# Expert weights in a routed two-layer network: one read and one kept copy of the last 64 rows of w1

## The chip, the core and the metric

The kernel runs on one core of a Trainium2 chip. The metric is device time in microseconds (us), the median over runs. The engines in the text are TensorE (PE, with its weight loads as PEld), VectorE (DVE), ScalarE (ACT), GpSimd (POOL) and SyncE (SP, which only issues transfers here). "DMA" is the core's 16 transfer engines together.

## The reference, cut to what matters

```
out  = causal 7-tap convolution of x per head (weights: softmax of `weight`)     # 28672 tokens x 192
logits = out @ w_gate                                                            # 8 experts
every token goes to one expert, greedily by logit, at most 3584 tokens an expert
for e in range(8):
    h = max(out[of e] @ w1[e], 0)        # w1[e]: 192 x 1024
    y[of e] = h @ w2[e]                  # w2[e]: 1024 x 192
```

All of it is float32. The kernel keeps float32 accuracy by splitting each operand in a high part (what TensorE's float32r format holds) and a low part (the rest), and by adding up several products of the parts.

## The kernel before

The program has two stages that overlap in time. First the convolution runs over 16 half batches (`conv`, tiles `X`, `cv`, `a`), its result is stored in DRAM (`attn`), and the gate's logits are formed (`aT`, `pl` or `bg`, `L`, `LT`). Then the two-layer network runs over 56 tiles of 512 tokens (`FFN.run`), while the routing of later tiles (thresholds, sorting, lists) goes on in the background, placed between the matmuls by a planner (`Pace`, `Steps.hook`), which counts a rough cost for each instruction that is written, and writes background steps where VectorE and ScalarE seem free.

A tile needs its expert's weights. `plan` writes the order of the pieces. The first eight tiles are one for each expert, and there each expert's weights are read from the inputs in eight pieces: `a` (rows 0 to 127 of w1, 512 columns at a time, two pieces), `d` (rows 128 to 191, two pieces), `w` (w2, four pieces). `wload` issues the read of one piece into one of four `raw` buffers. `wsplit` takes one piece: ScalarE writes the high part, VectorE (GpSimd for the four pieces that are split during the convolution) subtracts to get the low part, SP issues stores of both parts into DRAM (`kept1`, `keptd`, `kept2`; `kw`, `kd`, `kv` in the profile), and the read of the next piece is issued. So four pieces are under way at any time. Later tiles of the same expert do not split again: `W1` and `W2` read the kept parts back (16 times each), into the weight tiles `w1` and `dl` and into `w2` (the profile calls both weight tiles `w`).

The 64 last rows of w1 are held twice. TensorE's fourth matmul of a group has the high part of these rows in partitions 0 to 63 and again in 64 to 127 (`W[:, 2]`), because the moving operand `xd` has the tokens' high part in the lower half and their low part in the upper half. The fifth uses `dl`, the low part, whose upper half is zero. Before the change the doubling is done by reading the rows twice, into both halves of the `raw` buffer.

All transfers of weights are issued by SP, in the order in which they are written, each after what it waits for. The stores of `attn` are issued by ScalarE, gathers of tokens (`xg`) and scatters of results by GpSimd.

In a tile, step f does one group of five matmuls of layer one (`l1`, into one of three `ph` banks), ScalarE's `hh` and VectorE's `hl` empty the bank, then half a block of layer two of the tile before (`l2`), then one piece of `wsplit`.

Of the kernel before, what the change touches and what calls it, by code (L numbers as in the profile page):

```python
# [6 lines left out]
F32 = mybir.dt.float32  # L7
# [3 lines left out]
AF = mybir.ActivationFunctionType  # L11
# [4 lines left out]
NE, D, NTOK, F, CAP = 8, 192, 28672, 1024, 3584  # L16
W, HW_, NHB = 112, 16, 16
# [11 lines left out]
class Meter:  # L29


    def __init__(self, pace, name, eng):
        self.pace, self.name, self.eng = pace, name, eng
# [1107 lines left out]
class FFN:  # L1141
# [3 lines left out]
    def __init__(self, tc, nc, attn, w1, w2, out, ident, wr, drm):  # L1145
        self.tc, self.nc = tc, nc

        self.kept1 = [drm.tile([128, 3, F], F32, name="kw%d" % e) for e in range(NE)]
        self.keptd = [drm.tile([64, F], F32, name="kd%d" % e) for e in range(NE)]
        self.kept2 = [drm.tile([128, 8, 2 * D], F32, name="kv%d" % e) for e in range(NE)]  # L1150
        self.attn, self.w1, self.w2, self.out, self.ident, self.wr = attn, w1, w2, out, ident, wr
        self.bg = lambda: None
        self.busy = lambda: False
        self.WT, self.RAW, self.XG, self.XT, self.H, self.Y, self.XS = {}, {}, {}, {}, {}, {}, {}
        self.wpa, self.wpb, self.DL = [None, None], [None, None], [None, None]
        self.scat, self.late = [], []
        self.free = set()
        self.xg = None
# [31 lines left out]
    def wload(self):  # L1190
        nc = self.nc
        if self.loaded == len(self.pieces) or self.pieces[self.loaded][3] in ("W1", "W2"):
            return
        _, (e, _), _, what, q = self.pieces[self.loaded]
        t = self.wr.tile([128, 512], F32, name="raw")
        s = slice(512 * q, 512 * q + 512)
        if what == "a":
            nc.sync.dma_start(t, self.w1[e, 0:128, s])
        elif what == "d":
            nc.sync.dma_start(t[0:64], self.w1[e, 128:192, s])  # L1200
            nc.sync.dma_start(t[64:128], self.w1[e, 128:192, s])
        else:
            nc.sync.dma_start(t[:, 0:2 * D].rearrange("p (k d) -> p k d", d=D),
                              self.w2[e, 256 * q:256 * q + 256].rearrange("(k p) d -> p k d", p=128))
        self.RAW[self.loaded] = t
        self.loaded += 1

    def wsplit(self, i, eng):

        if self.done == len(self.pieces) or self.pieces[self.done][0] > i:  # L1210
            return
        V, A = self.nc.vector, self.nc.scalar
        _, ky, j, what, q = self.pieces[self.done]
        wp = self.wpa[j]
        e = ky[0]
        if what == "W1" or (what, q) == ("a", 0):
            W = wp.tile([128, 3, F], FR, name="w1")
            self.WT[ky] = [W[:, 0], W[:, 1], W[:, 2], self.DL[j]]
        if what == "W1":
            self.nc.sync.dma_start(W.bitcast(F32), self.kept1[e])  # L1220
            self.nc.sync.dma_start(self.DL[j][0:64].bitcast(F32), self.keptd[e])
            self.done += 1
            return
        if what == "W2":
            t = self.wpb[j].tile([128, 8, 2 * D], FR, name="w2")
            self.WT[ky].append(t)
            self.nc.sync.dma_start(t.bitcast(F32), self.kept2[e])
            self.done += 1
            return
        r = self.RAW.pop(self.done)  # L1230
        if (what, q) == ("w", 0):
            self.WT[ky].append(self.wpb[j].tile([128, 8, 2 * D], FR, name="w2"))
        t = self.WT[ky]
        if what == "w":
            r = r[:, 0:2 * D].rearrange("p (k d) -> p k d", d=D)
            s = slice(2 * q, 2 * q + 2)
            hi, lo = t[4][:, s, 0:D], t[4][:, s, D:2 * D]
        else:
            s = slice(512 * q, 512 * q + 512)
            hi, lo = (t[0][:, s], t[1][:, s]) if what == "a" else (t[2][:, s], t[3][0:64, s])  # L1240
        A.activation(hi, r, AF.Copy)
        n = 64 if what == "d" else 128
        eng.tensor_tensor(lo, r[0:n], hi[0:n].bitcast(F32), op=OP.subtract)
        S = self.nc.sync
        if what == "w":
            S.dma_start(self.kept2[e][:, s], t[4][:, s].bitcast(F32))
        elif what == "a":
            S.dma_start(self.kept1[e][:, 0, s], hi.bitcast(F32))
            S.dma_start(self.kept1[e][:, 1, s], lo.bitcast(F32))
        else:  # L1250
            S.dma_start(self.kept1[e][:, 2, s], hi.bitcast(F32))
            S.dma_start(self.keptd[e][:, s], lo.bitcast(F32))
        self.done += 1
        self.wload()

# [406 lines left out]
```

## Time and profile before

| what | value |
|---|---|
| median of 3 runs | 1273.2 us (1272.89 to 1273.23) |
| profiled execution, its time | 1268.0 us |
| span of the profile | 1266.2 us, mean granted TensorE clock 0.994 |
| busy in the span | PE 97%, DVE 79%, ACT 44%, POOL 40% |
| transfers | 193.02 MB in all, mean 152 GB/s; in the first quarter of the span 236 to 347 GB/s |

The profiled execution is 1.8 us longer than its span, and 5.2 us shorter than the median of the runs shown. The convolution takes the first 158 us; the eight tiles that split weights lie between 158 and about 323 us; from there to the end the kept weights are read back.

### The profile page before, as it was taken

How to read it: one execution, taken by the hardware profiler on the slowest of the kernel's cores; microseconds unless marked ns; L12 is line 12 of the kernel's file. 1: busy time of each engine (PE TensorE's matmuls, PEld its weight loads, DVE VectorE, ACT ScalarE, POOL GpSimd, SP SyncE). 2: the span in 40 equal slices, each digit the busy share in tenths (PEclk: the TensorE clock that was granted, in tenths of full speed). 3: DMA queues.
4: the chain of work that ended last, by engine and by line, in shares of the span. 5: the costliest groups of instructions: out<-in, count | busy, mean ns of one | idle time of the engine just before them, and what ended most of it. 6: DMA issues, size and time to landing. Idle time of an engine off the chain costs nothing.

```text
span 1266.2 us, 21792 instructions
## 1 busy us (share of the span) xinstructions
PE 1222.0 (97%) x7839; PEld 1049.9 (83%) x7839; DVE 999.6 (79%) x2245; ACT 551.2 (44%) x1220; POOL 510.1 (40%) x504
## 2 busy tenths in 40 slices
PE   5889979999999999999999999999999999999997
PEld 2445558899889888887889999999999999999997
DVE  7398669999999989988857777777777777777772
ACT  4544645565544543643433333333333333333332
POOL 3000435364444443533244444444444444444422
PEclk9999989999999999999999999999999999999999
DMA  9999897999533343423653513242314132231100
GB/s 236 347 334 297 271 328 257 294 316 319 194 103 112 122 152 94 152 93 125 161 126 105 205 41 100 94 155 62 129 48 147 46 102 97 85 105 47 45 26 28
DMA packets 100579, 193.02 MB, mean 152 GB/s; under 512 B 19232, under 2 KB 64752, under 8 KB 96240
## 3 DMA queue, kind: packets, MB, share of 16 engines
q1 hardware_dynamic: 57856, 115.15, 28.1%
q0 software_dynamic: 21504, 44.07, 11.7%
q10 hardware_dynamic: 21104, 32.34, 7.8%
q8 instruction: 63, 1.03, 0.3%
q14 instruction: 52, 0.43, 0.1%
HBM read 116.02 MB, written 75.50 MB: 151 GB/s over the span
## 4 chain that ended last, share of the span: by engine, by line
PE 83%; DVE 7%; DMA 5%; issue 1%; POOL 1%; ACT 1%; SPq 1%; POOLq 0%; ACTq 0%; DVEq 0%
PE ph L55 38%; PE y L55 37%; PE cv L55 3%; PE bg L55 3%; DMA X<-in_x_dram 1%; PE px L55 1%; DVE X L55 1%; DMA raw<-in_moe_w_dram 1%; DVE hl L55 1%; DVE oa L55 1%; DVE aT L55 1%; DMA wgr<-in_moe_w_gate_dram 1%; PE pl L55 1%; DMA X<-otab 1%; POOL xg L1262 0%
## 5 line engine op out<-in xcount | busy, mean ns | idle before, releaser
L55 PE MATMUL y<-w,hh 128*128 128x384 f32 x1792 | 539.3, 356 | 0.0
L55 ACT ACTIVATE hh<-ph 128x512 fp32r<-128x512 f32 x448 | 268.1, 598 | 494.2 <-PE ph L55 493.9
L55 PE MATMUL y<-w,hl 128*128 128x192 f32 x1792 | 448.9, 251 | 0.0
L55 DVE SCALAR_TENSOR_TENSOR hl<-ph,hh 128x512 fp32r<-128x512 f32 x448 | 308.1, 688 | 140.6 <-ACT hh L55 136.6
L55 PE MATMUL ph<-xa,w 128*128 128x512 f32 x1344 | 395.7, 402 | 3.9 <-DVE hl L55 3.9
L55 PEld LDWEIGHTS y<-w,hl 128*128 128x128 f32 x1792 | 341.0, 190 | 15.1
L55 PEld LDWEIGHTS y<-w,hh 128*128 128x128 f32 x1792 | 336.4, 188 | 19.1 <-issue 2.3
L1337 POOL DMA_INDIRECT out_dram<-yo,ib x128 | 127.9, 999 | 288.4 <-DVE yo L55 278.6
L55 PEld LDWEIGHTS ph<-xa,w 128*128 128x128 f32 x1344 | 218.7, 189 | 24.6 <-DVE hl L55 5.2
L1337 POOL DMA_INDIRECT out_dram<-yo,ia x96 | 112.2, 1168 | 262.3 <-DVE yo L55 230.0
L55 DVE STREAM_TRANSPOSE xs<-xg 32x256 f32<-32x256 f32 x496 | 182.9, 369 | 8.5
L55 PE MATMUL ph<-xd,w 128*128 128x512 f32 x448 | 177.3, 396 | 1.5 <-DVE xd L55 1.5
L55 PE MATMUL ph<-xd,dl 128*128 128x512 f32 x448 | 174.5, 390 | 0.0
L1262 POOL DMA_INDIRECT xg<-attn,jb x128 | 137.8, 1076 | 40.9 <-issue 40.9
L1262 POOL DMA_INDIRECT xg<-attn,ja x96 | 110.2, 1147 | 32.1 <-issue 26.7
L55 ACT ACTIVATE yt<-y 128x192 f32<-128x192 f32 x224 | 73.6, 328 | 102.6 <-PE y L55 99.5
L55 PE MATMUL cv<-X,TH 118*128 118x384 f32 x256 | 99.6, 515 | 18.9 <-DVE TH L55 12.5
L55 DVE TENSOR_TENSOR yo<-y,yt 128x192 f32<-128x192 f32 x224 | 79.4, 354 | 40.8 <-ACT yt L55 38.1
L55 PEld LDWEIGHTS ph<-xd,w 128*128 128x128 f32 x448 | 84.2, 188 | 21.2 <-DVE xd L55 2.0
L55 PEld LDWEIGHTS ph<-xd,dl 128*128 128x128 f32 x448 | 84.3, 188 | 19.7
L55 PEld LDWEIGHTS cv<-X,TH 118*128 118x128 f32 x256 | 44.6, 194 | 51.8 <-issue 13.0
L55 ACT ACTIVATE a<-cv 128x384 f32<-128x384 f32 x128 | 59.7, 492 | 53.3 <-PE cv L55 32.0
(237 smaller groups left out, 900.4 us busy)
## 6 DMA issues: line engine op xcount, KB each, us to landing
w<-kw SPq DMA_DIRECT2D x16, 1536.0 KB
w<-kv SPq DMA_DIRECT2D x16, 1536.0 KB
attn<-a ACTq DMA_DIRECT2D x16, 1344.0 KB
kw<-w SPq DMA_DIRECT2D x48, 256.0 KB
kv<-w SPq DMA_DIRECT2D x32, 384.0 KB
X<-in_x_dram SPq DMA_DIRECT2D x17, 672.0 KB
X<-in_x_dram ACTq DMA_DIRECT2D x15, 672.0 KB
raw<-in_moe_w_dram SPq DMA_DIRECT2D x32, 192.0 KB
```

Source lines behind the costliest of these rows:

```text
L55: return f(*a, **k)
L1262: self.nc.gpsimd.indirect_dma_start(out=t[:, b], out_offset=None, in_=self.attn[0:rows], in_offset=bass.IndirectOffsetOnAxis(ap=idx[b], ax ...
L1337: st = self.nc.gpsimd.indirect_dma_start(out=self.out, out_offset=bass.IndirectOffsetOnAxis(ap=idx, axis=0), in_=o, in_offset=None, bounds ...
```

## The change

The read of a `d` piece fills the lower half of the `raw` buffer alone: one transfer of 128 KB where there were two. ScalarE writes the high part twice, with two instructions of 64 partitions, to the lower and to the upper half of the weight tile, both from the lower half of `raw`. The store of the high part is of 64 partitions, into a second plane of `keptd`; `kept1` loses its third plane. The reload (`W1`) becomes four transfers in place of two: the two planes of `kept1` in one, the kept high part twice (into both halves), and the low part. The pieces `a` and `w` are as before: their loop over halves has one pass.

```diff
-        self.kept1 = [drm.tile([128, 3, F], F32, name="kw%d" % e) for e in range(NE)]
-        self.keptd = [drm.tile([64, F], F32, name="kd%d" % e) for e in range(NE)]
+        self.kept1 = [drm.tile([128, 2, F], F32, name="kw%d" % e) for e in range(NE)]
+        self.keptd = [drm.tile([64, 2, F], F32, name="kd%d" % e) for e in range(NE)]
...
             nc.sync.dma_start(t[0:64], self.w1[e, 128:192, s])
-            nc.sync.dma_start(t[64:128], self.w1[e, 128:192, s])
...
         if what == "W1":
-            self.nc.sync.dma_start(W.bitcast(F32), self.kept1[e])
-            self.nc.sync.dma_start(self.DL[j][0:64].bitcast(F32), self.keptd[e])
+            S = self.nc.sync
+            S.dma_start(W[:, 0:2].bitcast(F32), self.kept1[e])
+            for h in range(2):
+                S.dma_start(W[64 * h:64 * h + 64, 2].bitcast(F32), self.keptd[e][:, 0])
+            S.dma_start(self.DL[j][0:64].bitcast(F32), self.keptd[e][:, 1])
...
-        A.activation(hi, r, AF.Copy)
         n = 64 if what == "d" else 128
+        for q in range(0, 128, n):
+            A.activation(hi[q:q + n], r[0:n], AF.Copy)
         eng.tensor_tensor(lo, r[0:n], hi[0:n].bitcast(F32), op=OP.subtract)
...
-            S.dma_start(self.kept1[e][:, 2, s], hi.bitcast(F32))
-            S.dma_start(self.keptd[e][:, s], lo.bitcast(F32))
+            S.dma_start(self.keptd[e][:, 0, s], hi[0:64].bitcast(F32))
+            S.dma_start(self.keptd[e][:, 1, s], lo.bitcast(F32))
```

## Rows read from the trace of the kernel before

**Rows 1.** The page, part 1: busy time, share of the span, instructions.

```profile
PE 1222.0 (97%) x7839; PEld 1049.9 (83%) x7839; DVE 999.6 (79%) x2245; ACT 551.2 (44%) x1220; POOL 510.1 (40%) x504
```

**Rows 2.** Windows: from:to, length, busy per engine (count), clock, DMA share, GB/s.

```profile
166.00:184.00 18.00, 12.91 (x122) 8.86 (x120) 9.37 (x16) 7.36 (x17) 3.99 (x4) 0.72 1.01 347
184.00:200.00 16.00, 15.81 (x112) 13.73 (x113) 13.22 (x36) 6.79 (x16) 1.34 (x2) 1.00 0.64 223
200.00:320.00 120.00, 118.53 (x806) 105.81 (x805) 115.93 (x262) 71.73 (x157) 65.13 (x48) 1.00 0.94 306
...
368.00:376.00 8.00, 8.00 (x49) 7.31 (x48) 7.93 (x17) 2.96 (x6) 5.66 (x5) 1.00 0.88 278
```

**Rows 3.** Windows of 2 us, the first and last with a lowered clock.

```profile
172.00:174.00 2.00, 0.13 (x1) 0.13 (x1) 1.18 (x2) 1.01 (x2) 1.00 (x1) 0.80 0.98 333
...
182.00:184.00 2.00, 1.62 (x32) 1.12 (x24) 0.00 (x0) 0.30 (x2) 0.00 (x0) 0.64 1.02 352
```

**Rows 4.** The chain that ended last, 166 to 185: start, length, what.

```profile
166.87 7.25 DMA raw<-in_moe_w_dram
...
174.15 5.30 DMA raw<-in_moe_w_dram
```

**Rows 5.** Timeline of PE: start, length, tiles, count [idle before, releaser].

```profile
173.87 1.65 PE L55 MATMUL ph<-xa,w 128*128 128x512 f32 x3 [2.36 <-DVE hl L55]
...
176.31 2.79 PE L55 MATMUL bg<-aT,c_mu 128*32 128x128 f32 x48
180.47 0.47 PE L55 MATMUL bg<-ident,L 128*128 128x128 f32 x1 [1.37 <-ACT L L55]
180.87 2.75 PE L55 MATMUL bg<-aT,c_mu 128*32 128x128 f32 x48
```

**Rows 6.** Timeline of ACT in the same stretch.

```profile
177.63 0.63 ACT L55 ACTIVATE w<-raw 128x512 fp32r<-128x512 f32 x1 [0.38 <-DMA raw<-in_moe_w_dram]
178.17 0.58 ACT L55 ACTIVATE hh<-ph 128x512 fp32r<-128x512 f32 x1
179.47 0.63 ACT L55 ACTIVATE w<-raw 128x512 fp32r<-128x512 f32 x1 [0.72 <-DMA raw<-in_moe_w_dram]
```

**Rows 7.** Timeline of SP's queue in the same stretch.

```profile
174.15 0.60 SPq L1201 DMA_DIRECT2D raw<-in_moe_w_dram  x1
```

**Rows 8.** DMA issues of the whole span by tiles: count, size of one.

```profile
w<-kw SPq DMA_DIRECT2D x16, 1536.0 KB
...
kw<-w SPq DMA_DIRECT2D x48, 256.0 KB
...
raw<-in_moe_w_dram SPq DMA_DIRECT2D x32, 128.0 KB
dl<-kd SPq DMA_DIRECT2D x16, 256.0 KB
```

**Rows 9.** DMA of 160 to 180: the sum, and the queue of SP (q1).

```profile
DMA packets 3515, 6.66 MB, mean 333 GB/s; under 512 B 432, under 2 KB 1277, under 8 KB 3513
...
q1 hardware_dynamic: 2665, 4.48, 63.3%
```

**Rows 10.** ACT's groups by shape, whole span: busy, mean ns.

```profile
L55 ACT ACTIVATE w<-raw 128x512 fp32r<-128x512 f32 x32 | 20.0, 625 | 3.7 <-DMA raw<-in_moe_w_dram 3.7
L55 ACT ACTIVATE xd<-xs 64x512 fp32r<-64x512 f32 x31 | 19.2, 620 | 0.0
```

**Rows 11.** Timeline of ACT, one `d` piece: high part, then `hh`.

```profile
272.02 0.62 ACT L55 ACTIVATE w<-raw 128x512 fp32r<-128x512 f32 x1
```

**Rows 12.** Timeline of DVE, the same piece's subtraction.

```profile
272.67 0.68 DVE L55 TENSOR_TENSOR dl<-raw,w 64x512 fp32r<-64x512 f32 x1
```

**Rows 13.** Waits of DVE, 200 to 322: us in total, times, longest.

```profile
DVE w L55 <- ACT w L55: 0.8, 1, 0.8
```

**Rows 14.** Waits of ACT, 200 to 322.

```profile
ACT hh L55 <- PE ph L55: 32.0, 42, 1.6
```

**Rows 15.** Timeline of SP's queue: a reload and the next transfer after it.

```profile
681.46 0.34 SPq L1220 DMA_DIRECT2D w<-kw  x1
681.89 0.45 SPq L1221 DMA_DIRECT2D dl<-kd  x1
701.10 0.33 SPq L1227 DMA_DIRECT2D w<-kv  x1
```

**Rows 16.** Waits of SP's queue, 120 to 140.

```profile
SPq L1201 <- DMA attn<-a: 7.3, 1, 7.3
```

## The prediction

> **What bounds the kernel now.** I read the page first. TensorE is busy 97% of the span, so a change pays only where TensorE is idle or runs at its lower clock; the reader is to see that DVE, ACT and POOL have room in the mean [rows 1]. Then the windows. The pieces that the change touches are split from the end of the convolution to about 323 us. In that time there are three kinds of stretch. From 166 to 184 the transfer engines are full (share 1.01, 347 GB/s) and TensorE is busy 12.91 of 18 us at a mean clock of 0.72. From 184 to 200 it is busy 15.81 of 16. From 200 to 320 the transfers are nearly full (0.94), and yet TensorE is busy 118.53 of 120 us [rows 2]. So what can be won lies almost wholly in the 18 us from 166: 5.09 us of idle time and the cost of the clock. [...]
>
> Next the chain that ended last, in that stretch: two reads of raw weights make up most of it, 7.25 us from 166.87 and 5.30 us from 174.15 [rows 4]. The second read is issued at 174.15 by line 1201 [rows 7]: it is the upper half of the last `d` piece of expert 1, the very transfer that the change takes out. The timelines say how TensorE hangs on it. TensorE waits 2.36 us for `hl` before 173.87, runs a group and 48 small gate matmuls, and waits 1.37 us for `L` before 180.47 [rows 5]. ScalarE's queue is in order: it waits for the raw data of that piece until 179.47, writes its high part, and only then writes `L` [rows 6]. So a late raw piece stops TensorE through ScalarE.
>
> **The change part by part.** The reads: 32 transfers of 128 KB become 16. The stores: of the 48 of 256 KB to `kw`, the 16 of the `d` pieces become 128 KB [rows 8]. Together 16 x 128 + 16 x 128 KB = 4.2 MB of 193. Most of it is in the stretch where TensorE is full anyway, and is worth nothing there; the work that hides it is TensorE's own matmuls.
>
> In the 18 us the order of SP's queue says what is gone ahead of the last raw piece at 179.44: half the store of expert 0's second `d` piece, the second read of expert 1's first `d` piece, and the second read of the last piece itself, 3 x 131,072 bytes. Their price lies between two rates of the trace. All transfers together moved 333 GB/s from 160 to 180, which gives 0.39 us for 128 KB; SP's queue alone moved 4.48 MB in these 20 us, 224 GB/s, which gives 0.59 us [rows 9]. So the last raw piece comes 1.18 to 1.76 us earlier; as SP's queue has 63.3% of the transfer time, I take a value in the middle, 1.5 us. The issue of the removed transfer (0.60 us of SP) [rows 7] is not counted on top, since the data is late for 5.30 us after its issue: the queue of bytes is what is late, not SP.
>
> [...] No row here shows one store by itself.
>
> ScalarE gets a second instruction for each `d` piece. A write of 64x512 from memory to memory takes 620 ns, one of 128x512 takes 625 ns [rows 10], so halving the partitions saves nothing and the extra instruction costs its full 0.62 us, 0.54 us from start to start where another follows at once (177.63 to 178.17) [rows 6]. The extra one of the first piece falls into waits that ScalarE has anyway (0.38 and 0.72 us) [rows 6]. The extra one of the last piece stands right ahead of `L`, on the path: 0.54 to 0.62 us, say 0.6.
>
> So `L`, and TensorE after it, come 1.5 - 0.6 = 0.9 us earlier; from the ends 1.18 - 0.62 = 0.56 and 1.76 - 0.54 = 1.22. The wait of 2.36 us gets shorter too, by the 0.39 to 0.59 us of the halved store, but TensorE then only comes earlier to the wait for `L`, so this is not added. What is late next is the second round of the same gate work (48 matmuls, 2.75 us at the lower clock) [rows 5], which moves with it.
>
> In the following 120 us the 12 pieces of experts 2 to 7 have the extra 0.62 us, 7.4 us of ScalarE, which is busy 71.73 of 120 us [rows 2] and waits 32.0 us for TensorE ahead of `hh` alone [rows 14]. That wait hides it. If the cover were gone it would be VectorE that shows it: busy 115.93 of 120 us [rows 2], it is the engine with the least room. Its subtraction needs the lower half, which the first of the two instructions writes. If it has to wait for the second, up to 0.62 us is lost per piece where VectorE follows at once, as at 272.67 behind 272.02 + 0.62 [rows 11, 12]; but its waits for ScalarE's high parts in this stretch are one of 0.8 us [rows 13], so it mostly comes later than ScalarE. I put this at nothing. The two extra instructions in the convolution end behind a full TensorE as well, and are not counted.
>
> The planner sees the extra instruction as 0.49 us of ScalarE (0.12 + 512/1400) and may write a background step one place later. There are 1.47 us of TensorE idle from 200 to 320 [rows 2]: that bounds the gain, and I put as much for a loss. I take nothing.
>
> The reload: 1536 + 256 KB [rows 8] become 1024 + 3 x 256 KB, the same bytes, with two more issues (0.45 us each, as the 64-partition one has now). In the reload that has least time, the issue is at 681.46, and the next tile's second transfer, sent as that tile begins, is at 701.10 [rows 15]. A reload took about 8 us at 0.88 of the engines (368 to 376) [rows 2]. That leaves some 11 us; even if the 768 KB that now go in 64 partitions moved at half of the 278 GB/s, 2.8 us would be added to 8. Nothing.
>
> Sum: -0.9 us, against 1268.0 for the profiled execution (1266.2 span and 1.8 around it), so 1267.1. The median of the runs is 5.2 us above that execution, by what no view shows; I carry the difference over: 1273.2 - 0.9 = 1272.3. A measurement here can hardly tell less than 0.2% (2.5 us) from no change, so this is "the same".
>
> **The rivals.** First, it is faster: the fewer bytes clear the backlog, the 2.36 us wait shrinks so far that TensorE's clock does not fall, and the whole loss of this stretch goes. Idle time is 5.09 us [rows 2], and the second 48 gate matmuls take 2.75 us at the lower clock [rows 5], some half of it too much: 1.0 to 1.4. At most 6.5 us, 1266.7; in the middle, with half of it, 1270. For it: the chain is raw reads for 12.55 of 18 us [rows 4]. Against it: the store of `attn` and the gathers share the engines, and only 0.4 of 6.66 MB goes [rows 9].
>
> Second, it is slower: a wait of SP. One issue of line 1201 waited 7.3 us for a store of `attn`, which it neither reads nor overwrites [rows 16]. The order of issues changes with every transfer that is taken out or added, so such a wait can come to stand ahead of a raw read that TensorE hangs on. Where it was, it cost nothing. From a wait of 3.4 us in the 18 us on it decides (2.5 and the 0.9 won); with the full 7.3 us, 1273.2 - 0.9 + 7.3 = 1279.6. Against it: in the trace there is one such wait of that length.
>
> [...]
>
> **How the numbers follow.** The forecast, 0.9 us won (own range 1271.8 to 1273.0, and 1271 to 1273.5 with the planner's shifts), has a chance of 0.50; nothing won 0.13; the faster rival 0.23; the slower one 0.14. Faster by over 0.2% 0.23, within 0.2% 0.63, slower 0.14. The range goes into both outer cases: 1269.0 leaves out the lower half of the first rival, about 0.09, and 1276.0 most of the second, about 0.11.
>
> **What would show it.** Right: the second issue of the raw reads and line 1201 are gone; ScalarE has 16 more instructions of 64x512 at about 0.62 us; the wait for `L` still stands near 180 but ends about 1 us earlier; TensorE stays full from 200 to 320; no wait for a reload. Wrong: a granted clock of 1.00 from 166 to 184 (the first rival); an SP wait of some us for a store ahead of a raw read (the second); DVE waits for ScalarE's high part in most of the 14 pieces; or a TensorE wait for a `w<-kd` transfer after 323 us.

## The result, and the profile after

The changed kernel took 1278.63 us (median of 16 runs, 1275.33 to 1284.58) against 1273.07 us (16 runs, 1270.57 to 1278.47) of the kernel before, run beside it: a ratio of 1.0038, 95% interval 1.0026 to 1.0050, or 3.3 to 6.4 us slower; the two medians are 5.6 us apart. The forecast was 1272.3 us, the range 1269.0 to 1276.0. The profiled execution of the changed kernel took 1275.33 us (span 1273.6). It is the shortest of its 16 runs, so the profile shows less loss than the median.

The page after, part 1. As forecast, ScalarE has 16 more instructions, and 9.0 us more than in [rows 1]; TensorE's own work is hardly changed.

```profile
PE 1224.0 (96%) x7839; PEld 1049.3 (82%) x7839; DVE 1000.4 (79%) x2245; ACT 560.2 (44%) x1236; POOL 503.0 (39%) x504
```

The windows of [rows 2], after:

```profile
166.00:184.00 18.00, 12.31 (x132) 8.63 (x131) 11.77 (x21) 10.12 (x22) 4.59 (x5) 0.94 0.98 329
184.00:200.00 16.00, 16.00 (x112) 13.79 (x111) 13.44 (x37) 6.38 (x14) 1.53 (x2) 0.96 0.64 221
200.00:320.00 120.00, 115.39 (x784) 102.28 (x783) 111.72 (x248) 76.16 (x163) 55.46 (x47) 1.00 0.86 269
```

The start is no worse. From 200 to 320 us, where the forecast had TensorE full, it is idle 4.61 us instead of 1.47. The startup waits that answer to [rows 5] and [rows 6], on TensorE and ScalarE:

```profile
174.04 0.96 PE L55 MATMUL ph<-xa,w 128*128 128x512 f32 x3 [1.14 <-DVE hl L55]
...
180.47 0.33 PE L55 MATMUL bg<-ident,L 128*128 128x128 f32 x1 [3.14 <-ACT L L55]
```

```profile
178.68 1.28 ACT L55 ACTIVATE w<-raw 64x512 fp32r<-64x512 f32 x2 [0.18 <-DMA raw<-in_moe_w_dram]
179.99 0.22 ACT L55 ACTIVATE L<-bg 128x64 f32<-128x64 f32 x1
```

In the kernel before, the next row after the last one of [rows 6] is `L`:

```profile
180.00 0.21 ACT L55 ACTIVATE L<-bg 128x64 f32<-128x64 f32 x1
```

The two 64x512 writes stand right ahead of `L` and take 1.28 us where one took 0.63. From the start of the write to the start of `L` it is 1.31 us, where it was 0.53 (179.47 to 180.00). The DMA issues that answer to [rows 8] are those of the change:

```profile
w<-kw SPq DMA_DIRECT2D x16, 1024.0 KB
...
kw<-w SPq DMA_DIRECT2D x32, 256.0 KB
w<-kd SPq DMA_DIRECT2D x32, 256.0 KB
```

TensorE's waits over the whole span differ in two rows above all: three waits for `xa`, of up to 1.6 us, where the kernel before has one of 0.8, and one for `r_v` of 1.8 us, where it has none. Both are waits for VectorE.

```profile
PE px L55 <- DVE xa L55: 4.0, 3, 1.6
...
PE bg L55 <- DVE r_v L55: 1.8, 1, 1.8
```

VectorE and ScalarE in turn wait for TensorE, and part of that wait is not for its work. This is ScalarE's part of the same view:

```profile
ACT hh L55 <- PE ph L55: 433.1, 367, 2.9
...
ACT hh L55 <- issue: 25.2, 24, 1.8
...
ACT hh L55 <- remote: 7.2, 2, 4.9
```

For 26 `hh` the view finds nothing that let them go when they went. For 23 of them only the record is missing: they start 0.2 us after their fifth matmul (taken as its start + 0.25 us; TensorE's next matmul starts 0.22 us after it, the median of the 448 in this trace) and ScalarE's previous instruction, as most `hh` do in the kernel before too. The other three start 1.8 to 2.9 us after. One of these, with all three engines (start, length, what, [idle before]):

```profile
495.13 0.60 PE L55 MATMUL bg<-ident,r_wl 128*8 128x128 f32 x4
...
496.50 0.40 PE L55 MATMUL ph<-xd,dl 128*128 128x512 f32 x1
...
498.22 0.69 DVE L55 MAX8 r_s<-bg 8x8 f32<-8x512 f32 x1 [2.46 <-PE y L55]
...
499.66 0.60 ACT L55 ACTIVATE hh<-ph 128x512 fp32r<-128x512 f32 x1 [4.85 <-remote]
499.69 0.22 PE L55 MATMUL bg<-ident,r_v 8*128 8x8 f32 x1 [1.80 <-DVE r_v L55]
```

TensorE is done with `bg` at 495.73 and with the group of `ph` at about 496.9. VectorE, which reads `bg`, starts at 498.22, and ScalarE, which reads `ph`, at 499.66; both were idle. Then TensorE itself waits, for what VectorE makes of `bg`. In this document such an `hh` is called late when it starts over 0.4 us after both its fifth matmul (start + 0.25 us) and ScalarE's previous instruction are done. The trace has 13 late `hh`, 15.5 us together. The trace of the kernel before has none. The recorded updates of TensorE's semaphore agree with the starts: there is none between 498.19 and 499.64, and then six within 0.2 us, for matmuls that began between 496.50 and 497.64.

### The profile page after: what moved, and what is told of

It reads as the page before. It is cut to its first block, busy times and chain, and to the rows that moved or that the text cites. A ratio compares the mean times of both kernels' runs of the same rounds, so it can differ in the third digit from the quotient of the medians.

```text
span 1273.6 us, 21846 instructions
## 1 busy us (share of the span) xinstructions
PE 1224.0 (96%) x7839; PEld 1049.3 (82%) x7839; DVE 1000.4 (79%) x2245; ACT 560.2 (44%) x1236; POOL 503.0 (39%) x504
## 4 chain that ended last, share of the span: by engine, by line
PE 85%; DVE 8%; DMA 3%; issue 2%; ACT 1%; SPq 1%; another core or an unknown queue 1%; POOL 0%; POOLq 0%; DVEq 0%; ACTq 0%
PE ph L55 38%; PE y L55 37%; PE cv L55 4%; PE bg L55 2%; PE px L55 1%; DMA X<-in_x_dram 1%; PE pl L55 1%; DVE hl L55 1%; DVE X L55 1%; DVE aT L55 1%; DVE oa L55 1%; DMA wgr<-in_moe_w_gate_dram 1%; DVE w L55 0%; DMA raw<-in_moe_w_dram 0%
## 5 line engine op out<-in xcount | busy, mean ns | idle before, releaser
L1340 POOL DMA_INDIRECT out_dram<-yo,ia x96 | 106.8, 1112 | 274.4 <-DVE yo L55 237.1
L55 PE MATMUL cv<-X,TH 118*128 118x384 f32 x256 | 102.1, 524 | 17.3 <-DVE TH L55 12.4
L55 ACT ACTIVATE a<-cv 128x384 f32<-128x384 f32 x128 | 59.9, 492 | 55.6 <-PE cv L55 40.7
```

Source lines behind the costliest of these rows:

```text
L55: return f(*a, **k)
L1340: st = self.nc.gpsimd.indirect_dma_start(out=self.out, out_offset=bass.IndirectOffsetOnAxis(ap=idx, axis=0), in_=o, in_offset=None, bounds ...
```

## The experiments

Theories for the loss: the planner's order of the background steps (O), ScalarE's second instruction (S), the kept copies, that is their stores and the reload in four transfers (K). The figures are medians, and ratios to the kernel before run beside it, with their 95% intervals.

**The parts.** First each part alone. order_only is the kernel before, with this:

```diff
         n = 64 if what == "d" else 128
+        if what == "d":
+            self.nc.act += 0.12 + 512 / 1400
```

> The kernel before, with the planner alone told of 0.49 us more of ScalarE for each d piece, so that background steps are written in the order of the changed kernel; no instruction, transfer or byte is different. If the planner's order is the cause (O), this is about 5 us slower than before (1277 to 1280) and TensorE waits near 305 us for xa. If the second ScalarE instruction (S) or the kept copies and their reload (K) are the cause, it is within 0.2% of before (1271 to 1276).

Measured: 1268.12 us, ratio 0.9996 (0.9981 to 1.0011). uncharged is the changed kernel, with this:

```diff
+            act = self.nc.act
             A.activation(hi[q:q + n], r[0:n], AF.Copy)
+            if q:
+                self.nc.act = act
```

> The changed kernel, with the second ScalarE instruction hidden from the planner, so that the background steps stand in the order of before. O expects before's time (1272 to 1274); S and K expect the changed kernel's time (1277 to 1280), with a wait for c_bi or xa of over 1 us between 220 and 250 us as in the changed kernel.

Measured: 1266.88 us, ratio 0.9992 (0.9979 to 1.0005). reads_only is the changed kernel with the kept copies of before (`kept1` with three planes again, and so on):

```diff
-            S.dma_start(self.keptd[e][:, 0, s], hi[0:64].bitcast(F32))
+            S.dma_start(self.kept1[e][:, 2, s], hi.bitcast(F32))
...
-            S.dma_start(W[:, 0:2].bitcast(F32), self.kept1[e])
-            for h in range(2):
-                S.dma_start(W[64 * h:64 * h + 64, 2].bitcast(F32), self.keptd[e][:, 0])
+            S.dma_start(W.bitcast(F32), self.kept1[e])
```

> Read once and written twice by ScalarE as in the changed kernel; the stores and the reload as before (three planes of 128 partitions, two transfers). S and O expect the changed kernel's time (1277 to 1280). K expects before's time or up to 1 us less (1271 to 1274), and no hh of ScalarE that starts over 0.4 us after its matmuls and ScalarE's own last instruction are done.

Measured: 1267.66 us, ratio 0.9992 (0.9979 to 1.0006). kept_only is the changed kernel with the reads and the one ScalarE instruction of before:

```diff
             nc.sync.dma_start(t[0:64], self.w1[e, 128:192, s])
+            nc.sync.dma_start(t[64:128], self.w1[e, 128:192, s])
...
-        for q in range(0, 128, n):
-            A.activation(hi[q:q + n], r[0:n], AF.Copy)
+        A.activation(hi, r, AF.Copy)
```

> Read twice and written once by ScalarE as before; the high part is stored from 64 partitions and the reload goes in four transfers, two of them of 64 partitions of the same kept rows, as in the changed kernel. K expects the changed kernel's time (1277 to 1280) and late hh of ScalarE after reloads (some ten of 0.4 to 2.9 us). S and O expect before's time (1271 to 1275).

Measured: 1268.16 us, ratio 0.9994 (0.9981 to 1.0008).

None of the four differs from the kernel before, and none has a late `hh`. But uncharged is the whole change but for its order, and order_only is that order. And the kernel before, beside them, took 1268.79 us, 4.3 us less than in the first comparison. So the next question was whether the first comparison's difference belongs to the kernel at all (theory M: it does not).

**The same kernels again.** No edit.

> The changed kernel itself once more, beside the kernel before on one chip. If its parts only cost together (order of the background steps, second instruction and kept copies at once), it is again about 5 us slower than before here (ratio 1.003 to 1.005), with ScalarE's hh starting over 0.4 us late some ten times. If the 5 us and the late hh belong to the chip of the first comparison and not to the kernel (M), it is within 0.2% of before here (ratio 0.998 to 1.001), with at most one or two such hh, like its four relatives.

> The kernel before against itself: the ratio should be 1.000, and its distance from that is the error of one comparison of this size. If M holds and the chip is as it was for the four relatives, the profile has no late hh; if it is as in the first comparison, the kernel before has late hh too.

Measured: the changed kernel 1267.17 us, ratio 0.9993 (0.9982 to 1.0003), no late `hh`; the kernel before against itself 0.9990 (0.9978 to 1.0003), median beside it 1268.27. The same program that lost 5 us loses nothing here. Its window from 200 to 320 us is as full as in [rows 2], in spite of ScalarE's 78.60 us:

```profile
200.00:320.00 120.00, 118.43 (x803) 105.56 (x803) 114.82 (x260) 78.60 (x168) 58.65 (x48) 1.00 0.89 276
```

Its view of ScalarE's waits has no row of `hh` for "issue" or "remote"; they stand with TensorE's:

```profile
ACT hh L55 <- PE ph L55: 486.5, 415, 3.7
```

And at the place shown above all goes on at once:

```profile
492.20 0.60 PE L55 MATMUL bg<-ident,r_wl 128*8 128x128 f32 x4
...
492.84 0.69 DVE L55 MAX8 r_s<-bg 8x8 f32<-8x512 f32 x1
...
493.57 0.40 PE L55 MATMUL ph<-xd,dl 128*128 128x512 f32 x1
...
494.01 0.60 ACT L55 ACTIVATE hh<-ph 128x512 fp32r<-128x512 f32 x1 [2.13 <-PE ph L55]
...
494.89 0.22 PE L55 MATMUL bg<-ident,r_v 8*128 8x8 f32 x1
```

From TensorE's start on `bg` to VectorE's it is 0.64 us here and 3.09 us above. So what came late in the first comparison is the word from TensorE that it is done: its updates of the semaphore on which the others wait. ScalarE's word to VectorE is not late: in the trace after, all 448 `hl` start at most 0.04 us after `hh` and VectorE's previous instruction are done. I call a trace late or quiet by TensorE's updates.

**The suspected costs, enlarged.** Seven of the 13 late `hh` in the trace after are those of a tile's second group. So late_before and late_after make those of 19 tiles late, in both kernels alike. S2 is the theory that the changed kernel loses more by such lateness than the kernel before:

```diff
         nc.scalar.activation(hh[:, f], p, AF.Relu)
+        if f == 1 and 5 <= i < 24:
+            for _ in range(4):
+                nc.nc.scalar.activation(hh[:, f], p, AF.Relu)
```

> The kernel before, with hh of the second group of 19 tiles (tiles 5 to 23) written five times over, so that ScalarE is done with it some 2.2 us late 19 times, as in the first comparison's profile of the changed kernel, where the late hh mostly stand at that place. Output and the planner's order are unchanged. If such lateness is what cost time there, this is 4 to 20 us slower than before. It is the yardstick for the same edit in the changed kernel: if the changed kernel is more sensitive to lateness (S2), it loses over 3 us more there than here; if the first comparison's difference was its chip's alone (M), both lose the same within 2 us.

> The same edit in the changed kernel. S2: over 3 us slower than the kernel before with this edit. M: within 2 us of it.

ScalarE's second instruction five times over (act_x4), and more bytes ahead of the last raw piece (reads_x4):

```diff
             A.activation(hi[q:q + n], r[0:n], AF.Copy)
+        if what == "d":
+            for _ in range(4):
+                self.nc.nc.scalar.activation(hi[64:128], r[0:64], AF.Copy)
```

> The changed kernel, with the upper half of each d piece's high part written five times over in place of once: 4 x 0.54 = 2.2 us more of ScalarE for each of the 16 pieces, not told to the planner; the output is unchanged. By my argument the last piece of expert 1 puts 2.2 us ahead of L (the wait for L some 2 us longer), the two in the convolution cost nothing, and of the 12 from 200 to 320 us (26 us of ScalarE, which then is busy some 105 of 120) most is hidden: 2 to 5 us slower in all. If ScalarE's instructions there are not hidden (S), 10 to 26 us slower.

```diff
+            for n in range(3 * (e == 1)):
+                nc.sync.dma_start(self.more[3 * q + n], self.w1[e, 128:192, s])
             nc.sync.dma_start(t[0:64], self.w1[e, 128:192, s])
```

> The kernel before, with three copies of 128 KB each (from the same rows of w1 to a place in DRAM that nothing reads) issued ahead of the reads of the two d pieces of expert 1: six transfers more ahead of the last raw piece, twice what the change takes away. By my price (0.39 to 0.59 us for each) the last raw piece lands 2.3 to 3.5 us later and L and TensorE with it: 2 to 4 us slower. If the last raw piece is not late because of the bytes ahead of it, within 0.2% of before.

Measured: late_before 1286.80 us, 1.0087 (1.0056 to 1.0119); late_after 1297.32, 1.0154 (1.0125 to 1.0182); act_x4 1302.25, 1.0185 (1.0157 to 1.0212); reads_x4 1278.12, 1.0012 (0.9995 to 1.0029). The kernel before took 1276.50 us beside them, and all four traces are late. reads_x4 matters for that: it has none of the change, and has 16 late `hh`, 22.1 us. Its waits for `xa` are as long as those of the changed kernel (4.3 us in four). So M's first half holds: the late semaphores come without the change. Its second half fails: the changed kernel loses 10.5 us more than before by the same edit (S2). act_x4 is 25.8 us above the kernel before, and some 20 above what the changed kernel takes on such an occasion; that is what S expected, not the 2 to 5 of my argument. A part of it lies ahead of the pieces in question: tile 1 begins at 194.5 us there, and at 182.9 to 188.3 in the other 19 traces. act_x4 has no quiet run, so what it costs with updates on time is not known. The windows from 200 to 320 us, late_before, late_after and act_x4:

```profile
200.00:320.00 120.00, 116.47 (x791) 103.38 (x791) 112.80 (x254) 76.82 (x166) 62.87 (x47) 1.00 0.93 302
```

```profile
200.00:320.00 120.00, 109.83 (x716) 96.58 (x715) 102.50 (x228) 73.49 (x158) 49.21 (x41) 0.94 0.81 251
```

```profile
200.00:320.00 120.00, 110.61 (x759) 97.40 (x758) 102.45 (x228) 91.18 (x185) 44.88 (x40) 0.99 0.78 240
```

The 10.5 us of late_after over late_before are not waits alone. TensorE's granted clock is 0.94 in the mean in this stretch of late_after: it falls to its lower level, 0.50, for 3.4 us from 288.6 on (a mean of 0.58 in the 4 us below), after a wait of TensorE for `xa` of 1.9 us, and for 6.8 us from 312.5 on (0.57 in the 8 us below), in one of 3.2 us. At 0.50 in place of 1.00 these 10.2 us cost up to 5.1 us (an estimate from the two clocks and the two times).

```profile
288.00:292.00 4.00, 4.00 (x17) 3.52 (x16) 3.93 (x11) 0.00 (x0) 1.04 (x1) 0.58 0.60 193
...
312.00:320.00 8.00, 6.09 (x23) 5.53 (x24) 7.46 (x23) 2.50 (x7) 1.10 (x2) 0.57 0.83 268
```

reads_x4's price of a transfer stays open. Its last raw piece lands at 181.61, 2.8 us later than in late_before (178.79) and 1.5 later than in late_order (180.13); but in seven quiet traces with two reads the landing spreads from 178.48 to 181.10 by itself.

**Which part is sensitive.** The theories for the 10.5 us are again those of the parts: the order (O2), the second instruction (S2, from here on), the kept copies (K2). late_order, late_uncharged and late_kept put the three added lines of late_before into order_only, uncharged and kept_only:

```diff
+        if f == 1 and 5 <= i < 24:
+            for _ in range(4):
+                nc.nc.scalar.activation(hh[:, f], p, AF.Relu)
```

> The kernel before with hh of the second group of tiles 5 to 23 written five times over (as in late_before), and with the planner told of 0.49 us more of ScalarE for each d piece: the order of the changed kernel, none of its work. If the order of the background steps makes the changed kernel sensitive (O2), it loses about as much as late_after (1.015 where late_before has 1.009). If ScalarE's second instruction (S2) or the kept copies (K2) do, it loses as late_before.

> The changed kernel with the same late hh, its second ScalarE instruction hidden from the planner: all of the work of the change in the order of before. O2: like late_before (1.009). S2, K2: like late_after (1.015).

> The stores and the reload of the change alone (read twice, one ScalarE instruction, order of before) with the same late hh. K2: like late_after (1.015). O2, S2: like late_before (1.009).

> The changed kernel in the order of before, without any added lateness, beside the kernel before. On a chip like that of the first comparison (median of before 1273 or more, late hh in the profile) O2 expects a ratio of 0.999 to 1.001, S2 and K2 one of 1.003 to 1.005. On a chip like that of the four relatives all expect 0.999.

Measured, beside 1276.63 us, all traces late: late_order 1.0076 (1.0046 to 1.0105), late_uncharged 1.0182 (1.0142 to 1.0221), late_kept 1.0136 (1.0094 to 1.0177), uncharged_2 1.0023 (1.0001 to 1.0046). The order is out: order alone loses what late_before loses, the work in the old order as much as late_after. late_kept lies between; its interval overlaps those of late_before and late_after, so K2 is not settled by the times. uncharged_2 (no edit to uncharged) loses some 3 us where its first run, on a quiet occasion, lost none.

**The rest.** late_split4 puts the reload of late_before in four transfers, by the edit below. late_reads puts the added lines of late_before into reads_only; before_3 and kept_2 are the kernel before and kept_only again.

```diff
-            self.nc.sync.dma_start(W.bitcast(F32), self.kept1[e])
+            S.dma_start(W[:, 0:2].bitcast(F32), self.kept1[e][:, 0:2])
+            for h in range(2):
+                S.dma_start(W[64 * h:64 * h + 64, 2].bitcast(F32), self.kept1[e][64 * h:64 * h + 64, 2])
```

> The kernel before with the late hh of late_before, and with the reload of w1 in four transfers in place of two (two planes in one, the third in two halves of 64 partitions, the low part), from the kept copies as they were: same bytes, same stores, same reads. If the number of transfers of the reload makes the kept copies cost (K3), like late_kept (1.012 to 1.015); if their stores do, like late_before (1.009).

> Read once, written twice by ScalarE, order as changed, stores and reload as before, with the late hh. If ScalarE's second instruction costs what the kept copies don't (S2), some 5 us more than late_before (1.012 to 1.015); if the kept copies are all of it (K2), like late_before (1.009).

> The kernel before against itself: 1.000 within 0.2%. On a chip like that of the first comparison its profile has a dozen late hh as well (M2: the lateness is the chip's), and a TensorE wait for r_v near 495 us of at most 0.5 us; if it has none, the lateness comes from the change.

> The stores and the reload of the change alone, without added lateness. On a chip like that of the first comparison K2 expects 1.002 to 1.005 and the wait for r_v near 495 us of over 1 us; S2 expects 0.999 to 1.001. On a chip like that of the four relatives 0.999.

Measured, beside 1268.03 us, all traces quiet: late_split4 1.0069 (1.0049 to 1.0089), late_reads 1.0076 (1.0056 to 1.0095), before_3 1.0009 (0.9997 to 1.0021), kept_2 0.9998 (0.9985 to 1.0011). The occasion was quiet, so these four do not answer what they were made for. They do say that with quiet semaphores the added lateness tells a kernel with the second instruction from one without by little: late_reads loses 9.3 us and late_split4 8.3, where late_after lost 10.5 us more than late_before.

**All traces in one table.** Two stretches are measured on TensorE, from the start of the fifth matmul of tile 2's first group to that of tile 5's, and on to that of tile 8's (the added lateness begins in tile 5, after the first stretch). "Updates" counts the updates of TensorE's semaphore in the trace, and those that transfers made.

| kernel | before beside it | updates: TensorE, transfers | late `hh`, us | ScalarE instructions for a `d` piece | tile 2 to 5 | tile 5 to 8 |
|---|---|---|---|---|---|---|
| before | | 1259, 12172 | 0 | 1 | 65.3 | 58.5 |
| before_again | 1268.3 | 1262, 12162 | 0 | 1 | 65.1 | 58.6 |
| before_3 | 1268.0 | 1260, 12175 | 0 | 1 | 65.4 | 58.6 |
| kept_2 | 1268.0 | 1261, 12659 | 0 | 1 | 65.1 | 58.6 |
| uncharged | 1268.8 | 1261, 12417 | 0 | 2 | 65.3 | 58.6 |
| after_again | 1268.3 | 1257, 12411 | 0 | 2 | 65.4 | 58.6 |
| late_split4 | 1268.0 | 1259, 12692 | 0 | 1 | 65.3 | 59.4 |
| late_reads | 1268.0 | 1258, 11918 | 0 | 2 | 65.2 | 60.9 |
| reads_x4 | 1276.5 | 1160, 8383 | 16, 22.1 | 1 | 66.5 | 58.9 |
| late_before | 1276.5 | 1182, 8387 | 12, 14.5 | 1 | 66.2 | 60.0 |
| late_order | 1276.6 | 1168, 8465 | 13, 16.7 | 1 | 66.2 | 60.2 |
| late_kept | 1276.6 | 1167, 8647 | 16, 17.3 | 1 | 66.2 | 62.1 |
| after | 1273.1 | 1166, 8615 | 13, 15.5 | 2 | 67.6 | 59.9 |
| uncharged_2 | 1276.6 | 1167, 8350 | 15, 18.4 | 2 | 67.8 | 58.9 |
| late_uncharged | 1276.6 | 1172, 8630 | 17, 23.4 | 2 | 67.7 | 71.1 |
| late_after | 1276.5 | 1165, 8485 | 17, 20.5 | 2 | 69.0 | 71.2 |
| act_x4 | 1276.5 | 1168, 8519 | 12, 15.4 | 6 | 71.7 | 68.9 |

(The other three quiet traces, order_only, reads_only and kept_only, have 65.3, 65.3 and 65.3, and 58.6, 58.7 and 58.6.) While TensorE's updates are quiet, the second instruction costs nothing in tile 2 to 5: 65.1 to 65.4 with one or two. While they are late, tile 2 to 5 is 66.2 to 66.5 with one, 67.6 to 69.0 with two, 71.7 with six. The kept copies alone (late_kept) add nothing there. Every kernel with the second instruction also reads once, so these two are not told apart.

**Where tile 2 to 5 loses it.** It is tempting to put the 1.1 us between one and two instructions down to ScalarE's own time, some 0.8 us more for each of the six `d` pieces in this stretch. The rows say otherwise. This is the place in the trace after, and then in late_before:

```profile
210.22 1.20 PE L55 MATMUL bg<-oa,X 128*32 128x128 bf16 x32
212.59 0.60 ACT L55 ACTIVATE X<-bg 128x512 bf16<-128x512 f32 x1 [2.66 <-PE y L55]
214.30 0.36 DVE L55 TENSOR_TENSOR yo<-y,yt 128x192 f32<-128x192 f32 x1 [1.41 <-ACT yt L55]
223.14 0.69 PE L55 MATMUL bg<-oa,X 128*32 128x128 bf16 x16 [1.47 <-DVE c_bi L55]
```

```profile
209.60 1.19 PE L55 MATMUL bg<-oa,X 128*32 128x128 bf16 x32
210.36 1.21 ACT L55 ACTIVATE X<-bg 128x512 bf16<-128x512 f32 x2 [1.03 <-PE bg L55]
220.98 0.71 PE L55 MATMUL bg<-oa,X 128*32 128x128 bf16 x16 [0.73 <-DVE c_bi L55]
```

From TensorE's start on this `bg` to ScalarE's `X` it is 0.76 us in all eleven quiet traces, whether with one instruction or two, and in the four late ones with one. It is 1.70 to 2.38 us in the four late ones with two, and there ScalarE stands idle for 2.0 to 2.7 us before it. So what is late is one more update of TensorE; ScalarE is not behind with its second instruction. VectorE then waits 1.4 us for the `yt` behind this `X`, and TensorE twice as long for `c_bi`. Why this update comes late only in those four is not shown. The other wait of the stretch, for `xa` near 245 us, is 0.5 to 1.0 us in the quiet traces and 1.2 to 2.0 in all nine late ones, with the change or without.

act_x4 is another case: its ScalarE has no idle time before this `X`, and TensorE waits 2.2 us for `oa`. There it is ScalarE's own time that costs: 4 x 0.66 us more for each piece, 15.8 us in this stretch, and 2.7 to 4.1 us of TensorE.

## Why the prediction was wrong

**The step that failed** is the term put at nothing in "In the following 120 us": 7.4 us more of ScalarE, "That wait hides it". The 32.0 us of waits for TensorE [rows 14] were read from a quiet trace, and in quiet traces TensorE does stay full (118.43 of 120 us busy, after_again). In the trace after it is idle for 4.61 us there instead of 1.47. What the runs show in place of the cover is that TensorE's updates come up to 2.9 us late at `hh` in that trace, that ScalarE and VectorE stand idle until they come, and that TensorE then waits for VectorE. Tile 2 to 5 takes 67.6 us instead of 65.1 to 65.4. About half of that is lost by late kernels without the change too (66.2 to 66.5); the other 1.1 us or more come behind one more late update, which only the late kernels with the second instruction and the one read have. That ScalarE's time is what costs is shown for act_x4 alone, with five times the extra work; for the change itself it is not, and why it brings a late update more stays open.

**Behind it stands a second step**: "I carry the difference over". The profiled execution was 5.2 us shorter than the runs shown, "by what no view shows". It was not one of those runs: its 1268.0 us is below all 16 of the first comparison (lowest 1270.57). In three later comparisons the kernel before took 1268.0 to 1268.8 us, beside quiet traces; in the first it took 1273.1 and in two more 1276.5 and 1276.6, beside late ones. So the profile was of a quiet execution, and the runs that it was to predict are most likely of late ones. The difference was no constant that can be added to a sum; it was the sign that the trace did not show the conditions of the runs. The record names the chip of every comparison but the first: the two late ones ran on chip 13, the three quiet ones on chips 15, 8 and 0. So far lateness goes with the chip; with one chip late, twice, the chip and what ran beside it are not told apart.

**The startup.** The term of the extra instruction was a little too small: from the start of the write to `L` it is 1.31 us in place of 0.53, 0.78 us against 0.6. The 0.54 us from start to start were read where the next instruction begins 0.1 us before the write ends. In the trace after, all 16 second writes begin 0.02 us after the first has ended, and the next instruction 0.02 us or more after the second, so that a piece holds ScalarE for 1.30 us. The 1.5 us for the raw data can't be confirmed: over the seven quiet traces with two reads the last raw piece of expert 1 lands at 179.7 on average (178.48 to 181.10), over the four with one read at 179.3 (176.36 to 180.82), and `L` starts at 180.2 and at 180.6. The mean gain of 0.4 us is within that spread, and the extra instruction takes more than that. So the traces don't have the 0.9 us of the sum; the case that nothing is won, given a chance of 0.13, describes the startup best. The wait for `L` near 180 us is there, as said. What the halved store is worth is not shown: no run has a store by itself.

**The planner** was put at nothing, and it is nothing: 0.9996 quiet, and 1.0076 beside 1.0087 with made lateness. There is no TensorE wait for a `w<-kd` transfer either. Nor does the reload take the 2.8 us more that were allowed: from its first issue to the end of its last packet it is 9.21 us in the trace after and 8.75 in the kernel before (medians of 13 of the 16 reloads; behind the other three, SP's queue moves more within 16 us). But the reload, put at nothing because its data had 11 us to spare, is not without a mark. In the late traces TensorE waits for `r_v` some 7 to 10 us behind a reload, 0.27 to 0.40 us in the three with two transfers and 1.80 to 3.38 us in all six with four; in the quiet ones it does not wait, with two or with four. Here are the reload in the changed kernel, and the wait in late_before and in late_kept:

```profile
491.37 0.33 SPq L1220 DMA_DIRECT2D w<-kw  x1
491.75 1.09 SPq L1222 DMA_DIRECT2D w<-kd  x2
492.94 0.54 SPq L1223 DMA_DIRECT2D dl<-kd  x1
```

```profile
502.58 0.22 PE L55 MATMUL bg<-ident,r_v 8*128 8x8 f32 x1 [0.35 <-DVE r_v L55]
```

```profile
509.78 0.22 PE L55 MATMUL bg<-ident,r_v 8*128 8x8 f32 x1 [1.86 <-DVE r_v L55]
```

That four transfers hold TensorE's updates up longer than two fits this, and was not shown by a run of its own, since late_split4 ran on a quiet occasion. What it costs is not clear either. From tile 15's first group to tile 17's the changed kernel takes 43.1 us and reads_x4, with two transfers, 42.9; but uncharged_2, with four, takes 45.9. There the granted clock falls to 0.50 for 3.4 us (a mean of 0.57 in the 4 us below) after the wait for `r_v` (1.85 us, until 502.81), which in the trace after it does not do, after 1.80 us. The window in uncharged_2:

```profile
504.00:508.00 4.00, 4.00 (x16) 3.58 (x15) 3.93 (x13) 1.23 (x3) 0.57 (x1) 0.57 0.08 24
```

**The rivals.** The slower one was right about the direction, by luck: its mechanism was another (a wait of SP ahead of a raw read), and the late traces have late updates instead. The faster one's sign came half true without its gain: from 166 to 184 us the granted clock is 0.94 in the trace after and 0.84 in after_again, but it is 0.81 and 0.85 in two more traces of the kernel before, where [rows 2] has 0.72. It shifts from execution to execution, and no comparison shows a gain beyond what the kernel before has against itself. Between the two windows of [rows 3] the clock of the kernel before is 0.50 (174 to 182 us). The 1.0 to 1.4 us for the lower clock in the second 48 gate matmuls were too much as well: 48 of them take 1.94 us at a clock of 1.00 (from 175.39 on in the trace after), 0.8 us less than the 2.75. On a quiet occasion the forecast's "same" holds: 0.9993, with an error of about 0.1% by the kernel before against itself (0.9990, 1.0009).

**What stays open.** Of the 3.3 to 6.4 us, the trace after, set against reads_x4, places 1.1 us in tile 2 to 5 and 1.0 in tile 5 to 8; uncharged_2 has 1.3 and 0.0 there, and 3.0 in tile 15 to 17. The rest is not placed: the profiled run is the shortest of its 16, and no late trace of the kernel before without any edit was taken. The kernel before took 1273.1 us in the first comparison and 1276.5 on the late occasions, so how late its own updates were in the first is not known. How much of the loss is the kept copies' is open too, and so is whether the lateness would be there in executions of which no records are taken.

## What to carry to other kernels

Where the profiled execution is shorter than the timed runs by more than their spread, settle first what differs, since the idle time seen in the profile may not exist in the runs. A wait on a full engine is cover only as long as its semaphores come on time: here they came up to 2.9 us late at `hh`, and the full engine was idle for 4.61 us of 120. Before a loss is put down to an added instruction, look whether its engine was busy or idle ahead of the wait: here it was idle, and the update that it waited for was late. And before a difference of 0.4% is explained by the kernel, run the same two programs once more on another occasion: here the ratio was 1.0038 and 0.9993.

## What was not expected of the hardware

In nine of 20 traces TensorE's semaphore updates reached ScalarE up to 4.2 us after the matmul was done, in 12 to 17 places of 448; in eleven, of the same or nearly the same programs, not once over 0.4 us. The two kinds don't mix within a comparison. The late traces also hold fewer records: 1160 to 1182 updates of TensorE's semaphore against 1257 to 1262, and 8350 to 8647 updates by transfers against 11906 to 12692. VectorE's records are fewer as well (1439 to 1477 updates against 1684 to 1689), but in none of the traces without made lateness does an `hl` start late behind `hh`.

Missing records and late updates come in the same traces. No run here shows that the one is the cause of the other.
